# Filler products, another order of units in the opening stage, and earlier v casts for batch 1, in a fused sliding-window attention and GEGLU kernel

## Chip, core and metric

The kernel runs on one core of a Trainium2 chip. Five engines work from their own instruction queues: TensorE (PE) multiplies matrices into PSUM, VectorE (DVE), ScalarE (ACT) and GpSimd (POOL) work elementwise, SyncE (SP) issues most DMAs. They wait for one another through semaphores. The metric is the device time of one execution in microseconds (us). Before the change the median of five runs is 340.0 us (338.92 to 341.2).

## What is computed

Attention over 8 batches, 8 heads, 576 positions, 64 channels; heads 0 to 3 see the last 32 positions ("plain"), heads 4 to 7 every fourth of the last 128 ("dilated"). Its output, 4608 tokens by 512 channels, goes through a gated block with 1536 hidden channels:

```python
scores = scale * np.matmul(q, k.transpose(0, 1, 3, 2))
mask_plain = (rel >= 0) & (rel < window)                                        # window 32, heads 0-3
mask_dil = (rel >= 0) & (rel < window * dilation) & (rel % dilation == 0)       # dilation 4, heads 4-7
attn = softmax(np.where(mask, scores, -1e9))
x = (attn @ v) as tokens x channels
out = (gelu(x @ w_gate) * (x @ w_val)) @ w_out
```

## The kernel before, in words

**Work on two scales.** The gated block goes through the tokens in 9 chunks of 512 (`run_chunk`). A chunk has a first half (`gates[c]`, the products of `ffn1_part`, L586: gate and value weights for 12 blocks of 128 hidden channels, four products of 128x512 each, over the four 128-channel slices `kc` of x) and a second half (`outs[c]`, products with `wo`, L593). Attention works on 32 units `n`, four a batch, each a pair of heads; units 0 and 1 of batch 0 are plain, 2 and 3 dilated. A unit's result is one slice of `xT`, the transposed x that the gated block reads.

**Order by hand.** Nothing is scheduled by a tool: each engine runs its instructions in the order in which the program issues them, and `run_program` issues them from strings. A number n means n products of the chunk; a letter is one step of a unit: `c` cast of q or k of batch 0 (L349), `t` transpose on PE and copy out of PSUM (L364, L367; copy on DVE or ACT, L349, L345), `S` scores on PE (L432, in batch 0 with mask biases added first by L411), `P` exponential on ACT (L464), `M` mask multiply on DVE (L469, batches 1 and later), `D` row sums on PE with `two_ones` (L528), `T` and `B` the reciprocal of the sums on DVE (transpose L548, reciprocal L550, transpose back L565), `A` the same by logarithm and exponential on ACT (L557, L559), `N` the product of P and v on PE (L528, in batch 0 L526), `X` the division on DVE into `xT` (L578), `g` and `u` the Gelu on ACT (L733) and the product with the value half on DVE (L738). After `@` stands a PSUM bank or an index that selects one. "unit N4" below is step `N` of unit 4.

**The opening stage** is the part of `gates[0]` before its first number: all of batch 0's attention, with few products to put in between. Before it, `warm(12, 7)` runs 12 products of ones of 128x512 (L633). The first 16 products of a chunk have a written order, `firsts[c]`: three digits are block nb, gate (0) or value (1), and slice kc. In chunk 0 blocks 0 and 1 use banks 4, 5 and 6, 7, which also hold units N0 and N1 until X0 and X1 have read them. Slices kc 0 to 3 of `xT` come from X0 to X3.

**Batch 1's v.** `outs[0]` begins with `V1`, which calls `second_v`: on POOL it clears buffers (`zero`, L197, two memsets a view), casts the loaded v of batch 1 from float32 (`cast_v`, L253, four casts a view), and clears two further views. `views(2)` are batch 2's buffers: views 2 and 3 hold k, views 4 and 5 hold v (`vraw[2]`); the two blocks of `vraw[0]` cleared at the end are those of batch 3. The v of batch 1 arrives by SP's DMAs (L236, L242, L243), which wait for the second `wo` load. A view's four casts are two halves of the partitions (x) times two halves of the blocks (g); a plain unit needs one g of the plain view, with both x; a dilated unit needs both g of the dilated view, since its last block lies in the second.

Of the kernel before, what the change touches and what calls it, by code (L numbers as in the profile page):

```python
# [21 lines left out]
def kernel(  # L22
# [10 lines left out]
    nc = tc.nc  # L33
    B, H, S, D = q.shape
    NT, DM = out.shape
    DFF = moe_w_gate.shape[1]
    P = 128
# [14 lines left out]
    NB2 = S // BK  # L52
# [12 lines left out]
    ones = const.tile([P, CH], F16, tag="ones")  # L65
# [15 lines left out]
    vraw = [const.tile([P, 4 * NB2 * P], F16, tag=f"v{i}", name=f"v{i}") for i in range(3)]  # L81
# [7 lines left out]
    ps = psum.tile([P, 8, 512], F32, tag="ps")  # L89
# [86 lines left out]
    def blocks(t, plain):  # L176

        return t[:, (1 - plain) * 2 * NB2 * P : (2 - plain) * 2 * NB2 * P].rearrange("p (e c) -> p e c", c=P)

    def views(b):  # L180

        raw = qraw[b % 2]
        kt = raw[:, 1280 + 8 * NCL :]
        return (
            raw[:, 0:1280].rearrange("p (g c) -> p g c", g=2),
            raw[:, 1280 : 1280 + 8 * NCL].rearrange("p (g r i) -> p g r i", g=2, r=4),
            blocks(kt, 1),
            blocks(kt, 0),
            blocks(vraw[b % 3], 1),
            blocks(vraw[b % 3], 0),  # L190
        )

    def zero(t, eng=nc.gpsimd, half=(0, 1)):

        for x in half:
            part = t[64 * x : 64 * x + 64].bitcast(F32)
            eng.memset(part[:, :, 32 - 32 * x : 64 - 32 * x], 0.0)  # L197

    def st_of(i):
        return stage[:, 1280 * i : 1280 * i + 1280]  # L200
# [46 lines left out]

    def cast_v(dst, i):
        st = st_of(i)[:, 0:1152].rearrange("p (e d) -> p e d", d=D)
        for x in range(2):  # L250
            half = slice(64 * x, 64 * x + 64)
            for g in range(2):
                nc.gpsimd.tensor_copy(dst[half, NB2 * g : NB2 * g + NB2, half], st[half, NB2 * g : NB2 * g + NB2])  # L253

    def turn(dst, src):
        nc.sync.dma_start_transpose(out=dst, in_=src)
# [9 lines left out]
    def load_first(b):  # L266
        load_plain(q, b, 0)
        load_plain(k, b, 1)
        load_dil(q, b, 2)
        cast_plain(0, 0)  # L270
        cast_plain(1, 1)
        load_dil(k, b, 0)
        cast_dil(0, 2)
        cast_dil(1, 0)
# [326 lines left out]
    def store(c, tb, bank, eng):  # L601
        osb = osbp.tile([P, DM], F32, tag="osb")
        if eng == "act":
            nc.scalar.activation(osb, ps[:, bank, :], AF.Copy, bias=0.0, scale=1.0 / USCALE)  # L604
        else:
            nc.vector.tensor_scalar(osb, ps[:, bank, :], 1.0 / USCALE, None, ALU.mult)
        t0 = c * CH + tb * P
        nc.sync.dma_start(out=out[t0 : t0 + P, :], in_=osb)
# [22 lines left out]
    def warm(n, bank):  # L631
        for _ in range(n):
            nc.tensor.matmul(ps[:, bank, :], ones[:, 0:P], ones, start=True, stop=True)  # L633

    nc.vector.memset(two_ones, 0.0)
    for x in range(2):
        nc.vector.memset(two_ones[64 * x : 64 * x + 64, 64 * x : 64 * x + 64], 1.0)
# [30 lines left out]
    def second():  # L668

        load_w((4,))  # L670
        for t, src in ((0, q), (1, k)):
            nc.gpsimd.dma_start(out=six[:, t].rearrange("p h r d -> p h (r d)"), in_=sixes(src, 1))
        load_w((5,))
        load_eights(1)
        wo1 = [load_wo(i) for i in range(3)][1]
        two_masks()
        for t in views(1)[3:]:
            zero(t)
        tiles["two", 1] = views(1)
        gate["dma"] = wo1  # L680
        load_v(1, 1, True)
        load_v(1, 2, False)

    def second_v():
        for t in views(2)[2:]:
            zero(t)
        cast_v(views(1)[4], 1)
        cast_v(views(1)[5], 2)
        for t in blocks(vraw[0], 1), blocks(vraw[0], 0):
            zero(t)  # L690

    def gate_banks(c, nb):

        if c == 0 and nb < 2:
            return ((4, 5), (6, 7))[nb]
        low = ((0, 1), (2, 3))
        return low[(nb + c) % 2]
# [20 lines left out]
    def out_banks(c):  # L718
        return gate_banks(c, 2) * 2 if c < 7 else (4, 5, 6, 7)

    def run_program(c, words, mms, banks):

        units = {"S": two_s, "M": two_m, "D": two_den, "N": two_num, "T": two_t, "B": two_b, "X": two_x, "A": two_a, "P": two_p_of, "t": turn_first, "c": cast_six}
        for word in words.split():
            kind, args = word[0], [int(x) for x in word[1:].split("@") if x]
            if kind.isdigit():
                for _ in range(int(word)):
                    mms.pop(0)()
            elif kind in units:
                units[kind](*args)  # L730
            elif kind == "g":
                g = ffn.tile([P, CH], F16, tag="g")
                nc.scalar.activation(g, ps[:, gate_banks(c, args[0])[0], :], AF.Gelu)  # L733
                tiles["g", args[0]] = g
            elif kind == "u":
                nb = args[0]
                val = ps[:, gate_banks(c, nb)[1], :]
                nc.vector.scalar_tensor_tensor(u_all[:, nb, :], tiles.pop(("g", nb)), USCALE, val, ALU.mult, ALU.mult)  # L738
            elif kind in "ew":
                at = args[1] if len(args) > 1 else c  # L740
                store(at, args[0], out_banks(at)[args[0]], "act" if kind == "e" else "dve")
            elif kind == "L":
                mms.clear()
                last_block(c, 3, banks[3])
            elif kind == "V":
                second_v() if args else second()
            elif kind == "F":
                load_first(args[0])
            elif kind == "H":
                load_rest(args[0])  # L750
            elif kind == "R":
                load_rest(3)
                load_first(4)
                load_rest(4)
            elif kind == "E":
                nc.scalar.preload_act_table_set("natural_log_exp_and_others")
            else:
                nc.scalar.preload_act_table_set("gelu_and_others")
        assert not mms

    gates = {
        0: (
            "c0@0 c1@0 t0@0@1 t1@1@0 S0@4 P0 t4@0@1 c2@0 c3@0 t5@1@0 t2@2@1 t3@3@0 D0@0 T0 S1@6 t6@2@1 P1 S2@0 P2 "
            "t7@3@0 B0 D1@1 D2@2 A1 S3@2 N0@0 T2 X0 P3 D3@3 A3 N1@1 B2 X1 N2@2 X2 N3@3 X3 G V 16 g0 u0 g1 u1 8 g2 "
            "u2 8 g3 u3 8 g4 u4 8 g5 u5 8 g6 u6 8 g7 u7 2 t8@4@1 t10@6@1 6 g8 u8 2 t9@5@0 t11@7@0 6 g9 u9 2 "
            "t12@4@1 t14@6@1 6 g10 u10 2 t13@5@1 t15@7@0 6 g11 u11"
        ),
        1: (
            "3 N7@1 e3@0 1 X7 1 G 8 g0 3 g1 u0 3 u1 2 g2 4 u2 4 g3 4 u3 4 g4 4 u4 4 g5 4 u5 4 g6 4 u6 4 g7 4 u7 4 "
# [56 lines left out]
        6: "1 u11 12 e0@6 12 e1@6 12 e2@6 11",  # L826
    }
    firsts = {
        0: "000 010 100 110 001 011 101 111 002 012 102 112 003 013 103 113",
        1: "000 001 002 010 011 012 100 101 102 110 111 003 013 103 112 113",  # L830
        2: "002 003 000 012 013 010 001 011 102 103 100 101 112 113 110 111",
        3: "002 003 000 012 013 010 001 011 102 103 100 101 112 113 110 111",
# [48 lines left out]
```

## Time and profile before

| what | us |
|---|---|
| median of 5 runs | 340.0 (338.92 to 341.2) |
| the profiled execution's own time | 339.31 |
| its span, first to last instruction | 337.6 |
| PE busy in it | 328.9 (97%) |
| DVE, ACT, POOL busy | 165.4, 150.1, 147.0 |
| first product of the gated block (L586) | starts at 19.14 |
| unit N4 on PE | starts at 53.37 |

A timeline row reads: start, length, engine, line, operation, out<-in, shape, count of merged instructions, and in brackets the engine's idle time before it and what ended that. Matmuls overlap: one of 128x512 is shown with 0.38 us but the next starts 0.216 us later. The granted TensorE clock stands at 1.00 for the whole span.

### The profile page before, as it was taken

Reading aid. Unit: us, or ns where it says so; the run is one execution under the profiler, and the core shown is the slowest. Engines: PE = TensorE matmul, PEld = TensorE weight load, DVE = VectorE, ACT = ScalarE, POOL = GpSimd, SP = SyncE. Lnnn points to the kernel's source line nnn. Section 1 sums busy time; section 2 is a strip of 40 time slices with the busy share of each in tenths; the row PEclk is TensorE's granted clock in tenths of the full one; section 3 lists DMA queues with packets and bytes.
Section 4 is the critical chain, followed back from the end, with each engine's and each line's share of the span. In section 5 each row is a group of like instructions: output and inputs, shape, how many; then the busy total and the mean of one; then the engine's idle time right before and its main releaser. Section 6 shows DMA issues by size and latency. Waiting matters only on the chain.

```text
span 337.6 us, 6253 instructions
## 1 busy us (share of the span) xinstructions
PE 328.9 (97%) x2396; PEld 168.6 (50%) x2396; DVE 165.4 (49%) x258; ACT 150.1 (44%) x224; POOL 147.0 (44%) x253
## 2 busy tenths in 40 slices
PE   8799998999999999999999999999999999999996
PEld 3654554444644465446554465446544444444443
DVE  5773456443644365434893397736884024303320
ACT  1753563635763567346733563254433143223321
POOL 8776999575417648558647602681000000000000
PEclk9999999999999999999999999999999999999999
DMA  8999987996858799899889528971100110020002
GB/s 187 190 196 199 206 181 162 220 209 168 251 150 187 172 235 166 232 241 171 232 218 189 147 71 179 247 160 64 62 3 0 62 65 0 0 93 33 0 31 95
DMA packets 109022, 47.90 MB, mean 142 GB/s; under 512 B 83648, under 2 KB 104512, under 8 KB 108992
## 3 DMA queue, kind: packets, MB, share of 16 engines
q1 hardware_dynamic: 97216, 39.99, 50.0%
q0 software_dynamic: 11216, 6.79, 13.9%
q10 hardware_dynamic: 560, 0.72, 0.8%
q8 instruction: 19, 0.31, 0.4%
q14 instruction: 11, 0.09, 0.1%
HBM read 37.75 MB, written 9.44 MB: 140 GB/s over the span
## 4 chain that ended last, share of the span: by engine, by line
PE 83%; DMA 11%; SPq 2%; POOL 2%; issue 0%; DVE 0%; POOLq 0%
PE ps L586 49%; PE ps L593 25%; PE ps L528 6%; DMA wo<-in_moe_w_out_dram 4%; DMA wv<-in_moe_w_val_dram 3%; PE ps L432 3%; DMA stage<-in_v_dram 3%; DMA u_all<-in_q_dram 2%; SPq L236 1%; PE ps L617 1%; POOL v L253 1%; POOL wg L151 1%; SPq L242 1%; POOL wv L151 0%; POOL v L347 0%
## 5 line engine op out<-in xcount | busy, mean ns | idle before, releaser
L738 DVE SCALAR_TENSOR_TENSOR u_all<-g,ps 128x512 f16<-128x512 f16 x108 | 74.0, 686 | 107.0 <-PE ps L586 98.7
L733 ACT ACTIVATE g<-ps 128x512 f16<-128x512 f32 x108 | 64.3, 597 | 113.0 <-PE ps L586 112.9
L586 PE MATMUL ps<-xT,wg 128*128 128x512 f16 x432 | 114.5, 379 | 0.0
L586 PE MATMUL ps<-xT,wv 128*128 128x512 f16 x432 | 113.8, 379 | 0.0
L593 PE MATMUL ps<-wo,u_all 128*128 128x512 f16 x420 | 99.6, 379 | 0.0
L586 PEld LDWEIGHTS <-wv 128*128 128x128 f16 x432 | 41.8, 98 | 49.2
L586 PEld LDWEIGHTS <-wg 128*128 128x128 f16 x432 | 41.5, 97 | 48.4
L593 PEld LDWEIGHTS <-u_all 128*128 128x128 f16 x420 | 37.8, 98 | 38.8
L264 POOL COPY q<-dense 64x576 f16<-64x576 f16 (+2 forms) x70 | 39.1, 591 | 22.6 <-DMA dense<-s 19.1
L253 POOL CAST v<-stage 64x576 f16<-64x576 f32 x56 | 37.3, 691 | 1.9 <-DMA stage<-in_v_dram 0.6
L464 ACT ACTIVATE P<-ps 128x832 f16<-128x832 f32 (+1 forms) x32 | 26.6, 836 | 21.9 <-PE ps L432 21.7
L578 DVE TENSOR_TENSOR xT<-ps,rb 128x576 f16<-128x576 f32 x32 | 29.4, 933 | 9.7 <-ACT rb L559 5.4
L604 ACT ACTIVATE osb<-ps 128x512 f32<-128x512 f32 x34 | 20.2, 594 | 31.3 <-PE ps L593 31.3
L212 POOL CAST s<-stage 128x640 f16<-128x640 f32 x24 | 16.6, 721 | 38.1 <-DMA stage<-in_q_dram 25.9
L224 POOL CAST s<-stage 128x512 f16<-128x512 f32 x24 | 14.2, 618 | 10.1 <-DMA stage<-in_k_dram 4.8
L528 PEld LDWEIGHTS <-two_ones 128*128 128x128 f16 x176 | 13.9, 97 | 8.9 <-issue 1.0
L528 PEld LDWEIGHTS <-v 128*128 128x128 f16 x280 | 13.8, 98 | 6.8 <-POOL v L253 2.2
L528 PE MATMUL ps<-P,two_ones 128*128 128x64 f16 (+8 forms) x176 | 16.4, 227 | 0.8 <-ACT P L464 0.8
L528 PE MATMUL ps<-P,v 128*128 128x96 f16 (+1 forms) x280 | 14.8, 200 | 1.7 <-POOL v L253 1.7
L469 DVE TENSOR_TENSOR P<-P,two_d 128x768 f16<-128x768 f16 x14 | 8.8, 626 | 15.3 <-ACT P L464 15.3
L548 DVE STREAM_TRANSPOSE dt<-ps 128x576 f32<-128x576 f32 x20 | 15.4, 772 | 0.7 <-PE ps L528 0.7
L565 DVE STREAM_TRANSPOSE rb<-rc 128x576 f32<-128x576 f32 x20 | 15.4, 772 | 0.2
(68 smaller groups left out, 170.8 us busy)
## 6 DMA issues: line engine op xcount, KB each, us to landing
out_dram<-osb SPq DMA_DIRECT2D x35, 256.0 KB, 2.1
stage<-in_v_dram SPq DMA_DIRECT2D x32, 144.0 KB, 3.5
stage<-in_v_dram SPq DMA_DIRECT2D x28, 128.0 KB, 2.8
stage<-in_q_dram SPq DMA_DIRECT2D x24, 128.0 KB, 2.9
stage<-in_k_dram SPq DMA_DIRECT2D x24, 128.0 KB, 2.8
stage<-in_q_dram SPq DMA_DIRECT2D x6, 512.0 KB, 4.2
stage<-in_k_dram SPq DMA_DIRECT2D x6, 512.0 KB, 5.2
wg<-in_moe_w_gate_dram POOLq DMA_DIRECT2D x6, 256.0 KB, 8.1
```

Of the source, the lines that this page charges most:

```text
L212: nc.gpsimd.tensor_copy(s16[:, 1280 * t + 640 * g : 1280 * t + 640 * g + 640].rearrange("p (k c) -> p k c", k=5), st_of(i).rearrange("p (k ...
L253: nc.gpsimd.tensor_copy(dst[half, NB2 * g : NB2 * g + NB2, half], st[half, NB2 * g : NB2 * g + NB2])
L264: eng.tensor_copy(dst[half, :, :, half], src[half])
L464: nc.scalar.activation(pt[:, 0 : src.shape[1]], src, AF.Exp, bias=0.0, scale=scale)
L528: nc.tensor.matmul(o, lhs, rhs, start=st, stop=True, skip_group_check=True)
L548: nc.vector.transpose(dt.rearrange("p b c -> p (b c)"), psf[:, c0 : c0 + S])
L578: nc.vector.tensor_tensor(dst, num, rb, ALU.mult)
L586: nc.tensor.matmul(ps[:, bank, :], w[:, kc, ns], xT[kc][:, tok], start=first, stop=end)
L593: nc.tensor.matmul(ps[:, bank, :], u_all[:, fc, tb * P : (tb + 1) * P], wo_t[fc // 4][:, fc % 4, :], start=(fc == 0), stop=(fc == NNB - 1),)
L604: nc.scalar.activation(osb, ps[:, bank, :], AF.Copy, bias=0.0, scale=1.0 / USCALE)
L733: nc.scalar.activation(g, ps[:, gate_banks(c, args[0])[0], :], AF.Gelu)
L738: nc.vector.scalar_tensor_tensor(u_all[:, nb, :], tiles.pop(("g", nb)), USCALE, val, ALU.mult, ALU.mult)
```

## The change

Four edits.

- `idle` (letter `W`) is new: n products of ones of 128x160 into columns 352 to 511 of a bank, which no unit uses there. The opening stage gets five groups of them: 8 before S0, 5 before t5, 4 before S1, 4 before D1 and 10 before N1.
- In the opening stage t7 moves ahead of S2; S3 and P3 move ahead of N0; D2, T2 and A1 move behind N0 and X0. So on ACT P3 comes before the logarithm and exponential of A1, and on DVE X0 comes before T2.
- The first products of chunk 0 take the gate weights of blocks 0 and 1 for slices 0 and 1 first, then the value weights.
- In `second_v` the casts of batch 1's v come after the clears of k's views alone; the clears of `vraw[2]` follow the casts. In `cast_v` the four casts go g by g instead of x by x (in every batch).

```diff
     def cast_v(dst, i):
         st = st_of(i)[:, 0:1152].rearrange("p (e d) -> p e d", d=D)
-        for x in range(2):
-            half = slice(64 * x, 64 * x + 64)
-            for g in range(2):
-                nc.gpsimd.tensor_copy(dst[half, NB2 * g : NB2 * g + NB2, half], st[half, NB2 * g : NB2 * g + NB2])
+        for g in range(2):
+            at = slice(NB2 * g, NB2 * g + NB2)
+            for x in range(2):
+                half = slice(64 * x, 64 * x + 64)
+                nc.gpsimd.tensor_copy(dst[half, at, half], st[half, at])
...
+    def idle(n, bank):
+
+        for _ in range(n):
+            nc.tensor.matmul(ps[:, bank, 352:512], ones[:, 0:P], ones[:, 0:160], start=False, stop=True, skip_group_check=True)
...
     def second_v():
-        for t in views(2)[2:]:
+        for t in views(2)[2:4]:
             zero(t)
         cast_v(views(1)[4], 1)
         cast_v(views(1)[5], 2)
-        for t in blocks(vraw[0], 1), blocks(vraw[0], 0):
+        for t in views(2)[4:] + views(3)[4:]:
             zero(t)
...
-            "c0@0 c1@0 t0@0@1 t1@1@0 S0@4 P0 t4@0@1 c2@0 c3@0 t5@1@0 t2@2@1 t3@3@0 D0@0 T0 S1@6 t6@2@1 P1 S2@0 P2 "
-            "t7@3@0 B0 D1@1 D2@2 A1 S3@2 N0@0 T2 X0 P3 D3@3 A3 N1@1 B2 X1 N2@2 X2 N3@3 X3 G V 16 g0 u0 g1 u1 8 g2 "
+            "c0@0 c1@0 t0@0@1 t1@1@0 W8@7 S0@4 P0 t4@0@1 c2@0 c3@0 W5@7 t5@1@0 t2@2@1 t3@3@0 D0@0 T0 W4@7 S1@6 "
+            "t6@2@1 P1 t7@3@0 S2@0 P2 B0 W4@5 D1@1 S3@2 P3 N0@0 X0 D2@2 T2 A1 D3@3 A3 B2 W10@5 N1@1 X1 N2@2 X2 "
+            "N3@3 X3 G V 16 g0 u0 g1 u1 8 g2 u2 8 g3 u3 8 g4 u4 8 g5 u5 8 g6 u6 8 g7 u7 2 t8@4@1 t10@6@1 6 g8 u8 "
...
-        0: "000 010 100 110 001 011 101 111 002 012 102 112 003 013 103 113",
+        0: "000 100 001 101 010 110 011 111 002 102 012 112 003 013 103 113",
```

## The prediction, made before the changed kernel ran

> **What bounds the kernel now.** I read the page's busy times first, then PE's waits, then the timelines of PE, POOL, DVE and ACT in the two places where PE stood still. The page and the list of PE's waits:
>
> ```profile
> PE 328.9 (97%) x2396; PEld 168.6 (50%) x2396; DVE 165.4 (49%) x258; ACT 150.1 (44%) x224; POOL 147.0 (44%) x253
> PE ps L528 <- POOL v L253: 1.7, 1, 1.7
> PE ps L633 <- DVE ones L66: 1.5, 1, 1.5
> PE ps L432 <- DVE dense L349: 1.5, 2, 0.8
> PE ps L528 <- ACT P L464: 0.8, 3, 0.4
> ```
>
> PE is the bound, and its whole idle time inside the work is short: one wait of 1.7 us for a v cast, and some 2.3 us of small waits in the opening stage. After the v cast PE never waits again, so what moves PE there moves the end. PE and POOL around that wait:
>
> ```profile
> 49.81 1.89 PE L593 MATMUL ps<-wo,u_all 128*128 128x512 f16 x8
> 53.37 0.55 PE L528 MATMUL ps<-P,v 128*128 128x96 f16 x10 [1.66 <-POOL v L253]
> ...
> 46.09 2.40 POOL L197 MEMSET q<- 64x576 f32 x4
> 48.53 2.40 POOL L197 MEMSET v<- 64x576 f32 x4
> 50.99 5.60 POOL L253 CAST v<-stage 64x576 f16<-64x576 f32 x8
> 56.65 2.40 POOL L197 MEMSET v<- 64x576 f32 x4
> ```
>
> Eight products at 0.216 us (the step between the L586 rows below) end at 49.81 + 1.73 = 51.54; unit N4 starts at 53.37. So 1.83 us are lost (the 1.66 counts from the modelled end of the last product). N4 wants a clear and three casts of 0.66 to 0.99 us from POOL, which has been busy since 32 us and starts them after the clears of v. The chain of waits names a v load ahead of the casts, but POOL is idle for only 0.06 us before the first, so the clears set it.
>
> The opening stage (PE, then DVE, then ACT):
>
> ```profile
> 1.54 5.30 PE L633 MATMUL ps<-ones 128*128 128x512 f16 x12 [1.54 <-DVE ones L66]
> 9.17 0.56 PE L432 MATMUL ps<-q,dense 64*64 64x96 f16 x18 [0.85 <-DVE dense L349]
> 9.66 0.71 PE L367 MATMUL ps<-ident,xT 72*64 72x72 f16 x32
> 12.02 0.56 PE L432 MATMUL ps<-q,dense 64*64 64x96 f16 x18 [0.67 <-DVE dense L349]
> 17.80 1.41 PE L526 MATMUL ps<-P,v 64*64 64x96 f16 x60
> 19.14 0.39 PE L586 MATMUL ps<-xT,wg 128*128 128x512 f16 x1
> 19.37 0.38 PE L586 MATMUL ps<-xT,wv 128*128 128x512 f16 x1
> ...
> 10.41 1.55 DVE L349 COPY dense<-ps 128x576 f16<-128x576 f16 x3 [0.35 <-PE ps L367]
> 17.05 0.76 DVE L578 TENSOR_TENSOR xT<-ps,rb 128x576 f16<-128x576 f32 x1 [0.20 <-PE ps L526]
> 17.84 0.78 DVE L565 STREAM_TRANSPOSE rb<-rc 128x576 f32<-128x576 f32 x1
> 18.55 2.78 DVE L578 TENSOR_TENSOR xT<-ps,rb 128x576 f16<-128x576 f32 x3
> ...
> 16.51 0.81 ACT L464 ACTIVATE P<-ps 128x768 f16<-128x768 f32 x1
> 17.97 0.65 ACT L557 ACTIVATE lg<-ps 128x576 f32<-128x576 f32 x1 [0.65 <-PE ps L528]
> ```
>
> Here PE is not the bound: it waits for copies on DVE, which wait for PE's transposes. The last link is DVE's X0, B2, X1, X2, X3 from 17.05 to 21.33.
>
> **Part 1: the casts.** Clears of k end at 48.49, and the first cast can start there. Its loads: SP issues the four plain ones at 43.17, 43.81, 44.49 and 45.17 (chain of waits), and a load of this kind lands 3.5 us after its issue (list of DMA issues): 46.7, 47.3, 48.0, 48.7. With g ahead of x, N4 wants two casts, both of the first g: 48.53 + 2 x 0.66 = 49.9, or 50.5 at 0.99 each, the length of a cast that ran beside a mask multiply (DVE's at 51.00 took 1.06 instead of 0.56, so the two do hold each other). PE comes at 51.54 or later, so the wait goes: **-1.83**. What is late next: N5 wants the other plain casts, done by 51.2 to 51.8, and starts at 55.20 now; N6 wants all eight, done by 54.0 to 54.7 (8 x 0.68), and starts at 57.45. Both have over 1 us of cover with PE 1.83 earlier. The clears of v move behind the casts, to 54.1 to 56.5; the first user of those buffers is the cast at 72.36. The total on POOL is the same, so its next work, the cast at 59.11, stays. On SP the k loads wait for the plain casts (issued from 53.45): they can only come earlier. Batch 2 is tied to POOL: its last copy before S8 ends at 77.94 + 0.29 = 78.23, and S8 starts at 81.41, so PE may come 3.2 us earlier before that wait opens.
>
> **Part 2: the products of ones.** One of 160 columns costs 160/512 of 0.216 = 0.067 us, at the rate of the warm-up row ((6.64 - 1.54)/12 = 0.425) 0.133. The 31 cost 2.1 us or 4.1. W8 (0.54) lies in the gap of 0.85 before S0, which ends with DVE's copy: nothing. W4 before S1 (0.27) in the gap of 0.67: nothing. W4 before D1 (0.27): D1 waits for P1 on ACT anyway: nothing. Should these covers shrink, they cost at most their length. **W5 has no gap**: t4 and t5 are one unbroken row at 9.66 (x32), and DVE stood idle 0.35 us for t5. W5 delays t5 by 0.34, with two changes between half-height and full-height products some 0.45. Behind it on DVE are t5's copies and t3's; S1 waits for the last, so it goes from 12.02 to about 12.47. On the path: **+0.45**. The bounds are 0 (if t5's copy were late for another reason) and 0.75 (at the slow rate).
>
> What the products could buy is clock. All rows here show a granted clock of 1.00, and from 7.3 us on products of 512 columns step by 0.216. So in this trace there is nothing to win, and I take 0. The Trainium skill ("TensorE: Matmul & The Clock Gate", part 1, the HAM clock gate) says that PE falls to half rate after a mostly idle window of about 3.4 us, a window that runs freely, so that executions differ; the longest idle times here are 0.85 and 1.66 us. By that rule W buys nothing in any execution, the same sum; it speaks against this part of the change.
>
> **Part 3: the order.** From S1 0.45 later: P1 13.54 -> 14.0, P2 -> 14.75, D1 after P1 at 14.9. S3 no longer stands behind D2 (0.35), so it ends at 16.25 instead of 16.47, P3 runs 16.3 to 17.1, N0 ends at 16.8 and X0 starts there instead of 17.05. But T2 (0.77) and its reciprocal (0.27), which ran at 15.78 and 16.59 before X0, now follow it, and B2 and X1 behind them: 16.8 + 0.76 + 0.77 + 0.27 + 0.78 + 0.76 = 20.1 for the end of X1, against 18.55 + 0.72 = 19.27. On ACT, A1 follows P3: 17.05 + 0.65 + 0.68 = 18.4, A3's logarithm ends at 19.05; N3 reuses its banks, so N3 runs to 19.55. W10 (0.67) waits for X0, which read bank 5, and N1, N2, N3 follow it (0.41, 0.46, 0.47): 17.6 + 0.67 + 1.34 = 19.6, the same. So the gated block can start at about 19.6, but its second product (gate of block 1, bank 6) has to wait for X1: 20.15 against 19.37 for the second product now. **+0.8 at the entry to the gated block, W5's 0.45 included.** X2 and X3 end at 21.2 and 22.2 and are wanted at 21.7 and 22.55: covered. Bounds: +0.35 if W5 costs nothing; +1.4 with W5 and W10 at the slow rate; below nothing if executions exist in which the opening runs slowly and the products help, down to where the casts of N4 stop PE again: 51.54 - 49.9 = -1.6.
>
> **Part 4: gate weights first.** No wait for a weight load stands in PE's list, so it removes none; the value weights are wanted 0.4 us later relative to the first product. 0. Every weight load gains cover, as PE is 0.8 later.
>
> **Sum.** -1.83 + 0.8 = -1.0. The profiled execution took 339.31, so 338.3 on its footing. The median, 340.0, lies 0.7 above it and the five runs spread over 2.3 us. The profile does not say why; a POOL or DMA that is late before N4 would do it, and that the change takes off the path, so I carry only 0.2: **338.5 us** (-0.4%). About 0.5% (1.7 us, 338.3 to 341.7) is what can be told from no change.
>
> **Rivals.**
> - *The opening loses nothing or gains.* For it: five runs spread over 2.3 us, and I see one; in slow ones the products may hold the clock. Against: W5 and T2 stand in front of waiting work. Then 340.0 - 1.83 = 338.2 by the median or 339.31 - 1.83 = 337.5, at best 337.5 - 1.6 = 335.9.
> - *Stall gone, opening loses it all.* The opening loses 1.4 to 2.3, as both W5 and W10 run at the slow rate, or S8 opens: 339.3 + (-0.4 to 0.5) + 0.2 to 0.7, 339 to 341.
> - *The change does not do what it says at N4*: the v loads land far later than their 3.5 us. For it: they share the DMA engines with the last `wo` load. Against: the casts of before found them landed at 50.99. At 50.99 two casts end at 52.3, as PE comes (52.35), and the wait is gone still; to keep it whole they would have to land after 52. Then 339.31 + 0.8 = 340.1.
> - *Slower*: the opening, fuller of single products yet no faster, runs wholly at the slow rate up to the gated block. PE's busy time there (7.3 to 19.1, some 9.5 us, plus 2.1 of ones) would about double where it is not hidden. It decides from a loss of 1.83 in the opening; at 4 us it gives 342.
>
> **How the numbers follow.** Forecast 0.45, own range 337.6 to 339.4, two fifths of it under 338.3 (0.18 faster, 0.27 same). Opening free or better 0.22 (faster). Opening loses all 0.15 (same). Wait stays 0.10 (same). Slower 0.08. So faster 0.40, same 0.52, slower 0.08. The range leaves out the best of the second case and the worst of the last: 336.8 to 341.0.
>
> **What would show it.** Right: PE's list without the wait for L253, casts from 48.5, v clears behind them; W8 and both W4 inside gaps; t5 and S1 0.4 later; X1 ending near 20.1, and PE waiting for DVE's L578 before the second gate product; N4 near 52.3. Wrong: N4 still waiting; the first gate products at 19.2 or earlier; the granted clock under 1.00 in the opening; a wait at S8; a new wait of the gated block for weight loads.

## The result, and the profile after

The changed kernel takes 338.69 us (median of 39 runs, 337.75 to 340.27). The kernel before, run beside it, takes 339.26 (median of 70 runs, 338.44 to 341.28); the 340.0 of the five runs shown earlier was a high sample of it. The ratio is 0.9979, with a 95% interval of 0.9972 to 0.9986: 0.6 to 0.7 us faster, a real difference, but within the half per cent that the prediction could not tell from no change. The profiled execution of the changed kernel took 338.22 us with a span of 336.5, against 339.31 and 337.6.

First the busy times of the page, after the change:

```profile
PE 330.3 (98%) x2427; PEld 170.2 (51%) x2427; DVE 164.6 (49%) x258; ACT 150.2 (45%) x224; POOL 148.8 (44%) x253
```

PE has 31 instructions more, the products of ones, and is the bound as before. The list of PE's waits (columns: total, times, longest; what was a line from L253 to L633 in the kernel before is one higher here, the later ones six):

```profile
PE ps L634 <- DVE ones L66: 1.5, 1, 1.5
PE ps L527 <- issue: 0.7, 1, 0.7
PE ps L433 <- DVE dense L350: 0.7, 2, 0.4
```

The wait of 1.7 us for a v cast is gone, the waits before S0 and S1 are half as long, and a line is new: 0.7 us before a product of L527 (unit N0), where PE waits for nothing that the profile shows ("issue"). The place of the old wait, in the timelines of PE and then POOL:

```profile
50.56 1.89 PE L594 MATMUL ps<-wo,u_all 128*128 128x512 f16 x8
52.29 0.54 PE L529 MATMUL ps<-P,v 128*128 128x96 f16 x10
...
46.72 2.40 POOL L197 MEMSET q<- 64x576 f32 x4
49.18 6.28 POOL L254 CAST v<-stage 64x576 f16<-64x576 f32 x8
55.52 4.84 POOL L197 MEMSET v<- 64x576 f32 x8
60.42 2.71 POOL L212 CAST s<-stage 128x640 f16<-128x640 f32 x4
```

N4 starts 1.73 us after the first of the eight products ahead of it, with no gap, and the casts run straight behind k's clears. What the reader should also see is that POOL's row of casts has grown from 5.60 to 6.28 us and that the cast of L212, which began batch 2's chain at 59.11, now begins at 60.42.

The opening stage, PE and then DVE:

```profile
7.34 0.72 PE L639 MATMUL ps<-ones 128*128 128x160 f16 x8
8.35 0.56 PE L433 MATMUL ps<-q,dense 64*64 64x96 f16 x18 [0.29 <-DVE dense L350]
...
9.22 0.52 PE L639 MATMUL ps<-ones 128*128 128x160 f16 x5
...
11.77 0.56 PE L433 MATMUL ps<-q,dense 64*64 64x96 f16 x18 [0.39 <-DVE dense L350]
...
15.37 0.25 PE L527 MATMUL ps<-P,v 64*64 64x96 f16 x4
16.33 0.49 PE L527 MATMUL ps<-P,v 64*64 64x96 f16 x16 [0.71 <-issue]
...
19.70 1.23 PE L587 MATMUL ps<-xT,wg 128*128 128x512 f16 x4
...
16.86 0.76 DVE L579 TENSOR_TENSOR xT<-ps,rb 128x576 f16<-128x576 f32 x1 [2.28 <-PE ps L527]
17.54 0.77 DVE L549 STREAM_TRANSPOSE dt<-ps 128x576 f32<-128x576 f32 x1
18.34 0.27 DVE L551 RECIPROCAL rc<-dt 128x18 f32<-128x18 f32 x1
18.64 0.78 DVE L566 STREAM_TRANSPOSE rb<-rc 128x576 f32<-128x576 f32 x1
19.35 2.77 DVE L579 TENSOR_TENSOR xT<-ps,rb 128x576 f16<-128x576 f32 x3
```

N0 is now two rows, four products and sixteen, with a halt between them; X0 waits for it until 16.86, and the transpose of T2, the reciprocal and B2 stand in a row behind X0 and ahead of X1.

**The account of the two executions.** Three marks on PE: S0, the seventeenth gated product (the first behind the written order; I call it G17), and N4.

| | before | after | difference |
|---|---|---|---|
| S0 | 9.17 | 8.35 | -0.82 |
| S0 to G17 | 13.43 | 15.00 | +1.57 |
| G17 to N4 | 30.76 | 28.93 | -1.83 |
| N4 to the end of the span | 284.2 | 284.2 | 0 |

So all of it lies ahead of N4: the casts are worth 1.83, the opening costs 0.75. But the opening's cost is made of two parts of opposite sign. S0 came 0.82 earlier because PE's full rate began at 5.58 instead of 7.24 us in that execution. At these times the profile's record of the granted clock begins; ahead of them the warm-up products of 512 columns start 0.43 us apart instead of 0.216, which is half the rate. So the clock of 1.00 "for the whole span" leaves the start out. The start of the full rate differs from execution to execution: over the twelve profiles of this study it lies between 4.25 and 7.58, with and without the change. From S0 on, the changed opening is 1.57 longer.

### The profile page after: what moved, and what is told of

Same layout as the page of the kernel before. It is cut to its first block, busy times and chain, and to the rows that moved or that the text cites. A ratio compares the mean times of both kernels' runs of the same rounds, so it can differ in the third digit from the quotient of the medians.

```text
span 336.5 us, 6316 instructions
## 1 busy us (share of the span) xinstructions
PE 330.3 (98%) x2427; PEld 170.2 (51%) x2427; DVE 164.6 (49%) x258; ACT 150.2 (45%) x224; POOL 148.8 (44%) x253
## 4 chain that ended last, share of the span: by engine, by line
PE 97%; DVE 1%; issue 0%
PE ps L587 56%; PE ps L594 27%; PE ps L529 6%; PE ps L433 4%; PE ps L634 1%; PE ps L368 1%; PE ps L618 1%; DVE dense L350 1%; PE ps L527 1%; PE ps L639 1%; PE ps L412 0%; DVE xT L579 0%; PE ps L365 0%; DVE ones L66 0%; DVE osb L627 0%
## 5 line engine op out<-in xcount | busy, mean ns | idle before, releaser
L254 POOL CAST v<-stage 64x576 f16<-64x576 f32 x56 | 39.1, 698 | 3.3 <-DMA stage<-in_v_dram 0.4
L212 POOL CAST s<-stage 128x640 f16<-128x640 f32 x24 | 16.9, 732 | 33.2 <-DMA stage<-in_q_dram 21.6
```

The costliest lines, as they stand in the source:

```text
L212: nc.gpsimd.tensor_copy(s16[:, 1280 * t + 640 * g : 1280 * t + 640 * g + 640].rearrange("p (k c) -> p k c", k=5), st_of(i).rearrange("p (k ...
L254: nc.gpsimd.tensor_copy(dst[half, at, half], st[half, at])
```

## The experiments

In each, "before" is the kernel before, run on the same chip beside it. Of the fifth, seventh, ninth and tenth experiment there are only five runs each.

**1. The casts alone.** The kernel before with the changed `second_v` and `cast_v` only:

```diff
...
-        for t in views(2)[2:]:
+        for t in views(2)[2:4]:
             zero(t)
         cast_v(views(1)[4], 1)
         cast_v(views(1)[5], 2)
-        for t in blocks(vraw[0], 1), blocks(vraw[0], 0):
+        for t in views(2)[4:] + views(3)[4:]:
             zero(t)
```

> The kernel before with the cast part of the change alone (casts of batch 1's v ahead of the clears of v, g ahead of x). Theory A (the casts free PE, the opening's edits cost): the wait for the v cast is gone, first gate product at about 19.1 as before, N4 near 51.6, 1.8 us less than before: ratio 0.9946, faster than the full change by about 1.2. Theory B (the opening's edits cost nothing; the casts are worth only what the whole change shows): ratio 0.998, the same as the full change. Theory C (the 0.7 us in which PE waits for nothing that the profile shows, inside N0 in the changed kernel, belongs to a fixed place in PE's instruction stream, the 449th instruction): as in the profile of before the place is N0's last product, a gap of about 0.16 ahead of it, hidden by D3's wait for ACT.

Measured 337.96 us, ratio 0.9965 (0.9948 to 0.9982). S0 to S1 (2.85) and S0 to G17 (13.43) are those of the kernel before, G17 to N4 is 28.93 again, and N4 starts at 51.70. But the profiled span is only 0.7 shorter, not 1.8, and PE's list has a new line:

```profile
PE ps L433 <- POOL q L305: 0.8, 1, 0.8
```

It is unit S8, batch 2's first scores, which wait for POOL's last copy, and N4 to the end of the span is 285.2 instead of 284.2. PE and POOL there, from the timelines:

```profile
79.76 0.34 PE L433 MATMUL ps<-q 128*128 128x96 f16 x4
80.91 0.33 PE L433 MATMUL ps<-q 128*128 128x80 f16 x5 [0.80 <-POOL q L305]
...
48.62 6.27 POOL L254 CAST v<-stage 64x576 f16<-64x576 f32 x8
...
59.85 2.71 POOL L212 CAST s<-stage 128x640 f16<-128x640 f32 x4
...
77.65 2.85 POOL L265 COPY q<-dense 64x512 f16<-64x512 f16 x6 [1.74 <-DMA dense<-s]
80.57 0.29 POOL L305 COPY q<-q 128x128 f16<-128x128 f16 x1
```

Before, the copy stood at 77.94 and S8 came to it at 81.41. The row of casts is 0.67 longer, and the single casts of the trace say why. One that changes the half of the partitions starts 0.71 to 0.73 after the one before it, one that stays in the same half 0.60 to 0.61. Going x by x, two of a view's four stay in their half; going g by g, none do. Over two views that is 4 x 0.11 = 0.44; the rest is a second cast, stretched from 0.66 to 0.87, that overlaps DVE's mask multiply at 51.17 and its division at 52.29 (the first, at 1.00, has its like of 0.99 in the kernel before). Batch 2's chain starts 0.74 later, and its last copies wait 1.74 us for a transpose, for which they did not wait before. The chain of waits (start, length, what) gives the way from the late cast to the late copy:

```profile
60.51 0.73 POOL s L212
...
61.26 3.47 DMA stage<-in_k_dram
64.72 5.64 DMA dense<-s
```

and, behind POOL's next copies and casts, 1.73 us of waiting for the second transpose into `dense`. SP issued it 0.72 later than in the kernel before; the rows of SP before and in this experiment:

```profile
71.73 1.28 SPq L256 DMA_TRANSPOSE dense<-s  x1
...
72.45 1.25 SPq L257 DMA_TRANSPOSE dense<-s  x1
```

But it landed 5.1 us after its issue instead of 3.1 (list of DMA issues). Before, POOL could go on at 75.03 without a wait; here it goes on at 77.65. So the 2.6 at the end (77.94 to 80.57) are 0.7 of a later chain and some 2 of a slower transpose, and the cover before S8, 3.18 us, was eaten from both sides. What made the transpose slower the runs do not show; in the changed kernel (issued at 73.10) it landed after 3.1 again.

**2. The opening alone.** The changed kernel with the old `second_v` and `cast_v`; its diff to the kernel before is the changed strings and `idle`:

```diff
-            "c0@0 c1@0 t0@0@1 t1@1@0 S0@4 P0 t4@0@1 c2@0 c3@0 t5@1@0 t2@2@1 t3@3@0 D0@0 T0 S1@6 t6@2@1 P1 S2@0 P2 "
...
+            "c0@0 c1@0 t0@0@1 t1@1@0 W8@7 S0@4 P0 t4@0@1 c2@0 c3@0 W5@7 t5@1@0 t2@2@1 t3@3@0 D0@0 T0 W4@7 S1@6 "
...
-        0: "000 010 100 110 001 011 101 111 002 012 102 112 003 013 103 113",
+        0: "000 100 001 101 010 110 011 111 002 102 012 112 003 013 103 113",
```

> The changed kernel with the cast part undone, that is the opening's edits alone. Theory A: the second gate product comes 0.8 later than in before, relative to S0 some 1.5, but the wait for the v cast covers it: that wait shrinks from 1.8 to about 1.0 and the time is that of before, ratio 1.000. If the clears on POOL come late, 1.002 at most. Theory B: the same 1.000, with the wait as long as in before or longer (1.8 or more). Theory C: the 0.7 us inside N0 stands as in the changed kernel.

Measured 339.21 us, ratio 1.0005 (0.9993 to 1.0016): nothing. From the list of PE's waits:

```profile
PE ps L526 <- issue: 0.8, 1, 0.8
...
PE ps L528 <- POOL v L253: 0.6, 1, 0.6
```

The halt inside N0 is there again, G17 comes 15.21 after S0, 1.78 later than before, and the wait for the cast shrank from 1.7 to 0.6: while POOL is late at N4 anyway, most of what the opening loses (1.09, by G17 to N4) is absorbed there. That fits the opening alone costing nothing in time, and its cost showing only with the casts early (experiment 8).

**3. The changed kernel without the products of ones.** All five groups leave the strings:

```diff
-            "c0@0 c1@0 t0@0@1 t1@1@0 W8@7 S0@4 P0 t4@0@1 c2@0 c3@0 W5@7 t5@1@0 t2@2@1 t3@3@0 D0@0 T0 W4@7 S1@6 "
-            "t6@2@1 P1 t7@3@0 S2@0 P2 B0 W4@5 D1@1 S3@2 P3 N0@0 X0 D2@2 T2 A1 D3@3 A3 B2 W10@5 N1@1 X1 N2@2 X2 "
+            "c0@0 c1@0 t0@0@1 t1@1@0 S0@4 P0 t4@0@1 c2@0 c3@0 t5@1@0 t2@2@1 t3@3@0 D0@0 T0 S1@6 "
+            "t6@2@1 P1 t7@3@0 S2@0 P2 B0 D1@1 S3@2 P3 N0@0 X0 D2@2 T2 A1 D3@3 A3 B2 N1@1 X1 N2@2 X2 "
```

> The changed kernel without the 31 products of ones (order, gate weights first and casts kept). Theory A: t5 follows t4 at once, so S1 comes 0.4 to 0.5 earlier relative to S0 (3.4 in the changed kernel, 2.9 here). Theory C: with 62 instructions fewer ahead of it the 449th is D2's last product, not N0's fifth; N0 runs through and X0 starts some 0.7 to 1.1 earlier relative to S0 (8.5 in the changed kernel, 7.4 to 7.8 here). Together 0.7 to 1.1 us less than the changed kernel: ratio to before 0.995 to 0.996. If the products hold the clock up: the granted clock falls below 1.00 in the opening or products of 512 columns step by 0.43 there, and the time is that of the changed kernel or longer, 0.998 to 1.002.

Measured 338.21 us, ratio 0.9975 (0.9959 to 0.9990). PE's timeline from N0 on:

```profile
15.32 0.56 PE L527 MATMUL ps<-P,v 64*64 64x96 f16 x20
15.81 1.07 PE L529 MATMUL ps<-P,two_ones 128*128 128x288 f16 x12
17.36 1.51 PE L527 MATMUL ps<-P,v 64*64 64x96 f16 x60 [0.47 <-POOL v L348]
```

N0 runs through and X0 starts 7.44 after S0 instead of 8.51; S1 stands 3.24 behind S0 instead of 3.42; t5 waited 0.20 for the load of k here. In the next experiment, also without ones and without that wait, it is 2.85, as in the kernel before, so W5's own part is 0.57. G17 comes 13.93 after S0, 1.07 earlier than with the ones. In the medians the two kernels can't be told apart (0.9975 against 0.9979), and the 0.995 to 0.996 that was expected did not come. In this execution v of batch 0 landed late and N1 waited 0.47 for its cast, which takes back part of such a gain; whether that is so in the others is not shown.

**4. T2 back ahead of N0.** Also without ones:

```diff
-P3 N0@0 X0 D2@2 T2 A1
+P3 D2@2 T2 N0@0 X0 A1
```

> As the kernel without products of ones, and D2 and T2 moved back ahead of N0 and X0 (P3 and S3 stay ahead of N0). Theory A (T2 and its reciprocal behind X0 cost 1.0 on DVE): X1 follows X0 after B2 alone, 1.5 from X0's start to X1's start instead of 2.5; X0 starts about 0.4 later than without (D2 stands ahead of N0, and by theory C the 449th instruction is N0's last product). The second gate product 0.4 to 0.7 earlier than without this move; ratio to before 0.993 to 0.995. If the order costs nothing: the same as without the move, 0.995 to 0.996.

Measured 337.86 us, ratio 0.9967 (0.9956 to 0.9979). X1 starts 1.43 after X0 instead of 2.48, as DVE's transpose of T2 and the reciprocal run ahead of X0 again, and X0 comes 0.72 later. G17 stands 13.60 behind S0, 0.33 less. But S1, which lies ahead of this move, is 0.39 closer to S0 here (2.85 instead of 3.24); counted from S1, G17 comes at 10.75 here and at 10.69 without the move. N1 waited for v of batch 0 in both, 0.47 without the move and 0.15 with it, so the two are not a clean pair, but no gain of the move shows in them. In time the 0.35 us lie inside both intervals, and the 0.993 to 0.995 that was expected was missed.

**5. The casts alone, and the clears of v later still.** If the chain from POOL to S8 took back part of the gain, POOL should begin batch 2 earlier. The eight clears of v leave `second_v`, four go ahead of step `H` of batch 2 (its last loads) and four behind it:

```diff
         cast_v(views(1)[5], 2)
-        for t in views(2)[4:] + views(3)[4:]:
-            zero(t)
...
             elif kind == "H":
+                for t in views(2)[4:]:
+                    zero(t)
                 load_rest(args[0])
+                for t in views(3)[4:]:
+                    zero(t)
```

> The kernel with the cast part alone, and the eight clears of v taken out of second_v: four go ahead of batch 2's rest (after its q and k casts), four behind it. Theory D (the cast part's gain is given back in part at unit S8, whose q comes from POOL: the casts now run beside the mask multiplies and the eight clears stand between them and batch 2's casts): POOL's first cast of batch 2 starts at 57 to 58.5 instead of 59.85, its last copy ahead of S8 ends near 78.5 instead of 80.9, PE's wait of 0.8 for it goes, and the time falls by that: ratio to before 0.9940 to 0.9950 against 0.9965. If batch 2's path is set by its loads and not by POOL: the wait stays, 0.9965.

Measured 337.49 us, ratio 0.9942 (0.9928 to 0.9957): the best but one of the study, and below the kernel before and the changed one. POOL and PE from the timelines:

```profile
57.91 1.39 POOL L212 CAST s<-stage 128x640 f16<-128x640 f32 x2 [2.82 <-DMA stage<-in_q_dram]
...
78.00 0.29 POOL L305 COPY q<-q 128x128 f16<-128x128 f16 x1
...
79.86 0.51 PE L433 MATMUL ps<-q 128*128 128x96 f16 x9
```

Batch 2's chain starts 1.94 earlier than in the casts alone, the copy is done 1.6 us before S8 comes, and the wait of 0.8 is gone. In this execution the second transpose also landed 3.3 us after its issue, not 5.1, so how much of the gain at S8 is the clears and how much the quicker transpose, one trace of each does not tell. The times fit a wait that opens only in some executions: of the eleven of the casts alone four took 338.6 to 339.4 us, the profiled one among them, and seven 337.0 to 338.1; the five here took 337.15 to 337.76. The intervals of the two ratios overlap.

**6. Three warm-up products fewer.** The same kernel with nine instead of twelve. The question is whether time spent on ones ahead of the opening is wanted:

```diff
-    warm(12, 7)
+    warm(9, 7)
```

> As the last, with 9 products of ones at the start instead of 12. In the profiles so far PE reached full rate between 4.3 and 7.6 us, and S0 follows between 7.9 and 9.3. If PE's queue of warm-up products sets the entry, t0 comes 0.3 (early full rate) to 1.2 us (late) sooner, held then by the loads of t4 and t5 near 8.8 and 9.6: 0.3 to 0.8 less, ratio 0.992 to 0.994. If the shorter warm-up leaves PE at half rate for longer: products of ones and scores at twice the step until 8 to 11 us, 0 to 1 us more.

Measured 337.72 us, ratio 0.9962 (0.9944 to 0.9981), but it is two kinds of execution: six of twelve with a mean granted clock of 1.00 and a median of 337.25, and three with 0.984 to 0.988 and 338.7 to 340.2 (the other three lie between, 0.995 to 0.999). The profiled one was of the second kind. The page's row of the granted clock (forty slices of the span, tenths of full speed):

```profile
PEclk9589999999999999999999999999999999999999
```

Ahead of it PE's waits in the opening:

```profile
PE ps L433 <- DVE dense L350: 1.0, 2, 0.9
PE ps L368 <- DMA xT<-in_k_dram: 0.6, 1, 0.6
```

The clock stood at 0.50 from 9.47 to 19.71 us. The opening's products took longer (the 18 of S1 0.83 instead of 0.49 us), and G17 came 16.92 behind S0 instead of 14.19 in the fifth experiment. The window ahead of the fall is from 6.06 to 9.47, and busy times by window (PE is the first number behind the length) show what was different in it. This kernel:

```profile
6.06:9.47 3.41, 1.99 (x51) 1.52 (x49) 2.31 (x4) 1.57 (x3) 3.13 (x6) 1.00 1.24 207
```

The kernel before, first window of 3.41 us from the start of the full rate:

```profile
7.24:10.65 3.41, 2.56 (x76) 2.16 (x74) 1.94 (x4) 1.52 (x3) 2.72 (x6) 1.00 1.35 186
```

The changed kernel:

```profile
5.58:8.99 3.41, 3.12 (x55) 2.26 (x55) 2.39 (x5) 0.68 (x2) 3.17 (x6) 1.00 1.21 207
```

PE was busy for 58%, 75% and 91% of that window. I cut all twelve traces of this study into four such windows each from where the full rate begins: at full rate the lowest that was not followed by a fall is 67%, and the one of 58% is the only one that was. So the clock can fall in this opening, and the products of ones lift the first of these windows. It is one fall in one trace: 67% and 58% are what was seen, not a measured threshold.

**7. The same ones in fewer instructions.** The changed kernel with W8 and W5 as three products of 427 and two of 400 columns, both W4 left out, so that 16 products fewer are issued ahead of N0:

```diff
+        w = {3: 427, 2: 400}[n] if bank == 3 else 160
...
-            nc.tensor.matmul(ps[:, bank, 352:512], ones[:, 0:P], ones[:, 0:160], start=False, stop=True, skip_group_check=True)
+            nc.tensor.matmul(ps[:, bank, 512 - w : 512], ones[:, 0:P], ones[:, 0:w], start=bank == 3, stop=True, skip_group_check=True)
...
-t1@1@0 W8@7 S0@4
+t1@1@0 W3@3 S0@4
...
-W5@7 t5@1@0
+W2@3 t5@1@0
```

> The changed kernel with the same columns of ones ahead of S0 and t5 in 3 and 2 wide products (427 and 400 columns) instead of 8 and 5 of 160, and without the two groups of 4, which lay in gaps; the 10 before N1 stay. 32 PE instructions fewer ahead of N0. Theory C (the 0.7 us inside N0 stands at a fixed count of PE's instructions): the count now falls on D2's first product, N0 runs through, X0 starts 0.6 to 0.8 earlier relative to S0 (8.5 in the changed kernel, 7.8 here), while S1 stays 3.4 behind S0. Time 0.4 to 0.8 less than the changed kernel, ratio 0.9955 to 0.997. If the 0.7 us come from something else (N0's loads or its order): they stay inside N0, ratio 0.998.

Measured 338.12 us, ratio 0.9965 (0.9952 to 0.9978), as expected, but its interval overlaps that of the changed kernel (0.9972 to 0.9986).

```profile
14.92 0.56 PE L527 MATMUL ps<-P,v 64*64 64x96 f16 x20
16.61 0.85 PE L529 MATMUL ps<-P,two_ones 128*128 128x288 f16 x12 [1.13 <-ACT lg L558]
```

N0 runs through, X0 starts 7.63 behind S0, and the halt stands in front of the next unit, D2, where the count had put it. The profile puts it down to a logarithm on ACT, but D2 does not need that one: in the third experiment D2 starts at 15.81 and the logarithm at 16.24. Counted by products it is the same halt (see "Where the halt in N0 comes from"). T2 and X1 came late by it, and G17 stands 15.15 behind S0: moved, not removed.

**8. The changed kernel with the clears of v late.** The edit of the fifth experiment on top of the whole change:

```diff
         cast_v(views(1)[5], 2)
-        for t in views(2)[4:] + views(3)[4:]:
-            zero(t)
...
             elif kind == "H":
+                for t in views(2)[4:]:
+                    zero(t)
                 load_rest(args[0])
```

> The changed kernel with the eight clears of v moved as in the first of these four. In its profile PE stood no time at S8, but POOL's copy for it ended at 80.44 and S8's products ran from 80.32: no cover left. Theory D: in many executions S8 waits, and the 0.3 to 0.4 us by which the measured gain falls short of the predicted 1.0 lie there: ratio 0.9965 to 0.9975 against 0.9979. If S8 does not wait in the others either: 0.9979.

Measured 338.71 us, ratio 0.9974 (0.9955 to 0.9992): no different from the changed kernel. In its profile the copy of L305 ends at 78.83, one us ahead of S8 at 79.86, where the changed kernel's ends at 80.44, 0.12 after S8's start at 80.32. There was next to no wait at S8 to remove, because the changed opening brings PE there later. In this execution N0 had no halt and G17 came 14.10 behind S0; of the three profiles with this opening (the changed kernel, the second experiment and this one) two have the halt.

This kernel and that of the fifth experiment ran on the same chip and differ in the opening's edits alone. They took 338.71 us (11 runs, two of them under 338) and 337.49 (5 runs, 337.15 to 337.76). So with the casts early and the clears late, the changed opening costs 1.2 us of time in the medians; the intervals of the two ratios (0.9955 to 0.9992 and 0.9928 to 0.9957) only just touch. That is the plainest measure of the opening's edits in these runs: together they cost more than they bring.

**9. Nine warm-up products, and ones only in waits.** The sixth experiment's kernel with two groups of ones:

```diff
-t1@1@0 S0@4
+t1@1@0 W3@3 S0@4
...
-D0@0 T0 S1@6
+D0@0 T0 W2@3 S1@6
```

> The kernel of e6 (casts early, clears of v late, nine warm-up products) with two groups of products of ones put only where PE stands idle anyway: three of 427 columns before S0 and two of 400 before S1, so that the number of PE instructions ahead of N0 is 2 above that of before and the halt at the 449th stays at N0's end. In e6 three of twelve executions had a mean granted clock under 0.99 (0.984, 0.984, 0.988; 338.7 to 340.2 us) and the six at 1.00 a median of 337.25. Theory (the gate falls because PE is too idle in the opening, and the ones fill it): no execution of about twelve under 0.99, median 337.2, ratio to the kernel before about 0.994, the same as e6's undisturbed executions, since the ones lie in waits of 0.8 and 0.7 us and are 0.54 and 0.34 long. Rival (the fall is set by when the opening's waits meet the gate's window, and two groups of half a microsecond do not change that, or the wait for the k load of 0.6 us, which stays, is enough): two or more of twelve under 0.99 and a median of 337.5 to 338. Rival that the ones cost: 337.6 or more with the clock at 1.00 throughout, S1 more than 3.2 after S0.

Measured 337.53 us, ratio 0.9953 (0.9941 to 0.9966). None of the five executions had a clock under 0.99, one had 0.994: too few to say that the ones hold it. The rival on cost has a point, because of where the ones were put. PE's timeline:

```profile
11.55 0.50 PE L640 MATMUL ps<-ones 128*128 128x400 f16 x2 [0.67 <-DVE dense L350]
11.98 0.56 PE L433 MATMUL ps<-q,dense 64*64 64x96 f16 x18
...
16.26 0.51 PE L527 MATMUL ps<-P,v 64*64 64x96 f16 x17
17.14 0.22 PE L527 MATMUL ps<-P,v 64*64 64x32 f16 x3 [0.37 <-issue]
```

The second group went to bank 3, which t3's copy on DVE was still reading, so it waited out the gap that it was to fill and pushed S1 by 0.43. (Late loads of q and k held t4 and t5 by another 0.25 and 0.33 in this execution.)

**Where the halt in N0 comes from.** With five more products ahead of N0 and three fewer in the warm-up, the halt moved from N0's last product to its eighteenth. That is the pattern in every trace that has it: exactly 223 matmuls are recorded ahead of it, in the kernel before, the first and the tenth experiment (N0's last product, where the halt hides behind D3's wait for P3), in the changed kernel and the second experiment (N0's fifth), in the seventh (D2's first) and in the ninth (N0's eighteenth). What happens there is in the list of DMA queues, here of the changed kernel from 12 to 18 us (packets, MB, share):

```profile
q8 instruction: 1, 0.02, 1.5%
```

It is one transfer of 16 KB. In the trace it starts at 13.96 us in the kernel before, 13.42 in the changed one, 13.09 in the second and 13.75 in the seventh experiment, and PE goes on at 16.82, 16.33, 16.05 and 16.61; over all seven traces with the halt, 2.71 to 2.99 after the start. Where PE comes to the place late enough there is no halt: 2.92 after the start in the eighth experiment, 3.09 in the third, 3.40 in the fifth, 5.9 in the sixth. (In the fourth it passed at 2.67, so the step is not quite fixed.) What sets the start of the transfer is not shown. The place by count is shown, and it moved as forecast in the seventh experiment; that PE waits there for its own program is the reading that fits all of it. The Trainium skill ("Runtime: NRT & Kernel Launch", section on instruction fetch mechanics) says that the instruction memory is refilled in 16 KiB blocks and that crossing a boundary is mostly hidden; the block's size agrees with the queue's transfer, and in these traces the crossing is hidden where PE comes late or stands still for something else, while 0.71 and 0.79 us are bare in two of the three profiles of the changed opening.

**10. Gate weights first, alone.** The fifth experiment's kernel with the changed `firsts[0]`:

```diff
-        0: "000 010 100 110 001 011 101 111 002 012 102 112 003 013 103 113",
+        0: "000 100 001 101 010 110 011 111 002 102 012 112 003 013 103 113",
```

> The kernel of e5 (casts early, clears of v late, opening as in the kernel before) with only the order of chunk 0's first sixteen products changed, gate weights ahead of value weights. My theory (the order wins nothing, as no wait for a weight load stands in PE's list): 337.5 as e5, ratio 0.9935 to 0.995, first to seventeenth gated product the same 3.47 us apart as in e5, give or take 0.1. Rival (the value weights' loads or X1 hold the second and third product in some executions, and gates first frees them): 0.2 to 0.4 us less, 337.1 to 337.3. Other rival (both first products of block 1 need banks that X1 reads, so the second product waits for X1 0.4 longer): the seventeenth product 0.1 to 0.4 later relative to S0, 337.6 to 337.9.

Measured 337.16 us, ratio 0.9939 (0.9926 to 0.9953), against 0.9942 (0.9928 to 0.9957) without it. The first gated product and G17 are 3.63 apart, 3.47 in the fifth experiment: the second product, block 1's first, came 0.39 after the first instead of 0.23, as X1 ended only then. So in the trace the order costs 0.16 at its own place, and nothing that the runs resolve. Its 337.16 us is the lowest median of the study, 2.0 us below the kernel before in its own comparison, though not told from the fifth experiment's.

## Why the prediction was right, point by point

The prediction said 338.5 us, 336.8 to 341.0, most likely within 0.5%; it is 338.69 and 0.2% faster. Its likeliest case, the stall gone and the gated block entered 0.8 later, is what the profiled execution shows. The first half of that is right by its mechanism. The second came out by luck: measured from S0 the opening lost twice as much, and an early S0 made up for it. By its own steps:

- **The casts, -1.83: right at N4.** G17 to N4 fell from 30.76 to 28.93 in nine of the ten kernels with early casts (the fifth experiment's has 29.42, PE having waited for a load of `wo` ahead of 47.69). The two casts of the first g were done long before PE came.
- **"Its next work, the cast at 59.11, stays" and the cover of 3.2 us before S8: wrong.** The cast moved to 60.42 and the last copy from 77.94 to 80.15. "The total on POOL is the same" is the sentence that failed: casts that go g by g change the half of the partitions each time and cost 0.11 more for two of each four, and one more of them is stretched. The rest of the 1.3 is POOL coming to the casts 0.63 later behind a longer opening. And a shift of POOL does not pass unchanged through loads and transposes: in the casts alone 0.74 became 2.6, with a transpose that landed 2 us later after its issue. In that profile, with the opening unchanged, the wait at S8 opened (0.8 us). In the changed kernel PE arrives so late that it just does not. This was inside the range's second case ("S8 opens").
- **W5, +0.45: right in kind, a little small.** S0 to S1 grew from 2.85 to 3.42, +0.57, and without ones it is 2.85 again (fourth experiment). The 0.34 of the products is sound; the 0.11 put down for the two changes of height had no row behind it, and 0.23 is what is left for them.
- **The other ones, 0: wrong by a mechanism the step did not have.** W8 and the two W4 did lie in waits. But as instructions they are not free: with them, less the six products of D2 that went behind N0, the place of the halt came 15 products earlier, out of D3's wait and into N0, 0.71 us bare. The third and the seventh experiment, with no ones and with fewer, show that it moves with their number; the eighth's profile, with all of them and no halt, that it is not bare in every execution.
- **The order: right in its numbers by luck.** X0 at 16.86 (predicted 16.8), end of X1 at 20.07 (20.1), second gated product at 20.12 (20.15), N4 at 52.29 (52.35). These agree because two things that the sum lacked cancelled in that execution: the earlier S0 (-0.82) and the halt in N0 (+0.71). The +0.8 for the entry is +1.57 when counted from S0: W5's 0.57, the halt's 0.71, and 0.29 left for T2 behind X0 and its row of DVE work, where the sum had 0.35.
- **Clock, 0 and "W buys nothing in any execution": not shown wrong for the changed kernel's time, but the reason was.** The rule that it cited speaks of an idle window ("mostly" is the prediction's word); the sixth experiment lost the clock after a window in which PE was busy for 58%, and the measurement decides. What the ones buy is a margin: in that first window PE was busy for 75% in each of the six profiles with twelve warm-up products and no ones, and for 91% to 97% in the four with W5 and W8 or their wide form. Of 67 executions of the kernel before that stand beside these experiments four had a mean clock of 0.990 (339.6 to 340.0 us), of the 39 of the changed kernel none was under 0.995. That leans to a gain in the rare execution and does not prove one; in the medians the changed opening only costs (eighth against fifth experiment).
- **Gate weights first, 0: right** within what the runs resolve.
- **Carrying only 0.2 of the 0.7 between the median and the profiled execution: right result, idle reason.** The kernel before has its median at 339.26, at its profiled execution's 339.31, so there was nothing to carry. The sum of -1.0 was 0.3 to 0.4 too large, and the 0.2 that should not have been there hid half of it. The changed kernel's median lies 0.5 above its own profiled execution, which had an early S0. From S0, the three profiles with this opening lose 1.57, 1.78 and 0.67 before G17, the last one being the one without the halt; against the 1.83 of the casts that leaves gains of 0.26, 0.05 and 1.16, and the measured 0.6 to 0.7 lies between them. That fits a halt that comes in some executions and not in others; how often it comes is not shown.
- **The rivals.** "Opening free" fell: with the clears late the changed opening costs 1.2 us (eighth against fifth experiment), and the trace has it 1.57 longer. (The casts alone, 0.9965, and the whole change, 0.9979, have intervals that overlap.) "Opening loses all" was nearer than its 0.15 said: in the profile it lost 1.57 of 1.83, counted from S0. The late loads and the slow rate did not occur in the changed kernel's profile; the slow rate did with three warm-up products fewer, for 10 us, and cost 1.5 to 3 us (338.7 to 340.2 against 337.25).

## What to carry to other kernels

When work on one engine is put ahead of other work, follow the late work to its last consumer and let every shift pass through the DMAs between; here 0.7 us of longer casts, with a slower transpose on the way, became 2.6 us at a copy 20 us later, and with eight clears that nobody yet needed moved out of the way the copy came in time. Filler instructions are not free because they lie in a gap: count them as well as their time, since here 21 of them, less six products that went the other way, moved a halt of 0.7 us from under another wait into the open. Look for "issue" in the list of waits, and for a wait on something that the product does not need. (Fewer, longer fillers moved the halt again, but did not shorten the opening here.) Before adding fillers for the clock, cut the trace into windows from where the full rate begins and read PE's busy share in each: here one of 58% was followed by a fall, and none of 67% or more. And test each part of a change alone: without its opening this one would have gained about 1.8 us instead of 0.6, given the clears late.

## What was unexpected of the hardware

- Casts on POOL that go from one half of the partitions to the other start 0.71 to 0.73 us apart, in the same half 0.60 to 0.61. A row of four in batch 2 shows it too: 2.61 us x by x, 2.83 g by g. Early casts with the old order inside a view were not tried.
- PE halted at one place of its program, behind the 223rd recorded matmul, in seven of twelve traces, until 2.71 to 2.99 us after a 16 KB transfer of the instruction queue had started, bare for up to 0.8 us.
- The granted clock fell to 0.50 after a window of 3.41 us with PE busy for 58% and no single wait over 0.85 us, and came back only after three such windows with PE busy for 94% to 100% (9.47 to 19.71 us), while at the start of a run PE reached the full rate 2.7 to 6.0 us after its first product.
- When the full rate begins differs by up to 3.3 us between executions (4.25 to 7.58 us), and S0 with it by 1.5 (7.87 to 9.34). A difference of a microsecond between two profiles can be this alone, so marks are better measured from S0 than from the start of the span.
